# Load tiles moved by 128 bytes, and every load one chunk on two rings

## The chip, the core and the metric

The kernel runs on one core of a Trainium2 chip. The metric is the device time of one execution in microseconds (us). A core has five engines with instruction streams of their own: TensorE (PE, with PEld for its weight loads), VectorE (DVE), ScalarE (ACT), GpSimd (POOL) and SyncE (SP), which only issues transfers here. A transfer (DMA) is issued by an instruction on an engine's queue (SPq, ACTq) and is carried out by 16 DMA engines that all queues share. SyncE's and ScalarE's issues go into a ring each.

## The reference

Four inputs `q`, `k`, `v`, `alpha` of shape (4, 8, 768, 48) in fp32 are 4 batches of 8 heads, 768 steps and 48 numbers. A recurrence over the steps gives `y`, and a mixture of low-rank adapters is added to it:

```
for t in range(S):
    state = alpha[:, :, t, :, None] * state + einsum('bhd,bhe->bhde', k[:, :, t], v[:, :, t])
    y[:, :, t] = einsum('bhd,bhde->bhe', q[:, :, t], state)
x = y.transpose(0, 2, 1, 3).reshape(3072, 384)
logits = x @ w_gate                      # 8 experts, the best two are kept, softmax over them
delta = sum over the two: w * ((x @ A[e]) @ B[e])      # rank 16
return x + delta
```

## The kernel before

**Units.** The work is cut into 24 units: unit u is chunk c = u % 6 (128 steps) of batch b = u // 6, all 8 heads. For a unit ScalarE takes the logarithm of alpha (`ln`), TensorE sums it along the chunk (`cum`), ScalarE exponentiates (`exp`), GpSimd multiplies k and q by that (`kg`, L381) and casts v (`vb`), TensorE transposes (`tr`), ScalarE copies the result out of PSUM (`kq`), TensorE forms the 128x128 attention blocks (`at`), VectorE masks them (`msk`, L412), TensorE multiplies by v and by the state (`av`, `kv`; VectorE scales the state, `st`), ScalarE copies y (`ysb`, L454), TensorE transposes it (`xt`), ScalarE casts it (`xs`). Then groups of one to three units go through the gate: `z`, a chain of small VectorE steps, `zt`, `zs`, and for each unit `dl` and `o` (VectorE adds, L559), after which the unit is stored.

**Order.** The order of all these steps is fixed when the program is built: `_order` plays a list schedule with a cost for each step (`_ops`), a priority for each (`PRIO`, `PERIOD`) and an arrival time for each loaded piece (`_arrivals`). No clock exists when the kernel runs: each engine takes its instructions in that order and waits for semaphores.

**Loads.** `_plan` lists the loads. Batch 0 is loaded by chunk: 24 pieces of 128 steps x 8 heads x 48 numbers, 196,608 bytes each. Batches 1 and 2 and `a`, `k` of batch 3 are loaded whole, 10 loads of six such pieces; `q` and `v` of batch 3 by chunk again. `load` (L266) issues one. Three of the first six go to ScalarE's ring, all others to SyncE's; the three weight loads (`W_st`, `G_st`, `B_st`) come after the 16th load. There are two buffers of each tile (`a_t`, `kq_t`, `v_t`), so a load of batch 2 waits for the readers of batch 0 (`pump`, L569). Stores are issued on SyncE once no load is left in the queue.

**Where the rows lie.** In SBUF a head's 48 numbers (192 bytes) have a slot of 64 numbers (256 bytes), so rows start 256 bytes apart. In the built program `a_t0` begins at byte 16,512 of each partition, which is 64.5 x 256, and the other load tiles follow at multiples of 256 behind it. So each row fills bytes 128 to 319 counted from a multiple of 256: it crosses one such multiple. `W_st` begins at 151,680 (592.5 x 256). It too is loaded in rows of 192 bytes, eight per partition, but these lie one behind the other: they start at 128, 64, 0 and 192 from a multiple of 256, twice over, and half of them cross one. In DRAM the rows of the inputs and of `moe_A` are 192 bytes apart.

**Completion counters.** The framework merges the engines' streams into one order and gives the DMAs in it eight completion counters in turn (`DMAHW0` to `DMAHW7`). A DMA is issued only when the one eight before it in that order, which had the same counter, has landed. At most eight transfers are under way, and an engine whose next instruction is such a DMA waits with all that stands behind it.

Of the kernel before, what the change touches and what calls it, by code (L numbers as in the profile page):

```python
# [18 lines left out]
NCH = S // C  # L19
# [13 lines left out]
LNS = [[0], [1]] + [[u, u + 1] for u in range(2, NU, 2)]  # L33
CAST = set()


# [19 lines left out]
def _pe(t):  # L56
    return t + .22, t


SMALL = (.17, .13)  # L60
KEEP = dict(lg=2, ex=3, kg=4, kt=4, am=3, sb=2, vb=4, xs=9)
SLOTS = dict(C=1, A=1, M=3)
PRIO = dict(ln=5.1, cum=-1.8, exp=10.2, kg=-0.6, vb=2.0, tr=1.7, kq=2.4, at=3.7, msk=-1.3, st=10.4,
            kv=4.1, av=2.5, ysb=17.0, xb=5.0, xt=10.1, xs=-6.3, z=13.4, gm=7.3, df=8.3, ge=8.9,
            gx=19.3, wu=5.0, dn=4.8, w=-0.1, zw=16.1, zt=7.3, zs=20.8, dl=12.7, o=3.4)
PERIOD = 2.6
SLACK = 0.


def _ops(arr):  # L70
    ops = {}

    def add(name, eng, length, deps, war=(), alloc=None, frees=None):
        ops[name] = (eng, length, list(deps), list(war), alloc, frees)

    gof = {u: g for g, us in enumerate(GROUPS) for u in us}
    lof = {u: us for us in LNS for u in us}
    for i, us in enumerate(LNS):
        war = [("cum", u) for u in LNS[i - KEEP["lg"]]] if i >= KEEP["lg"] else []
        add(("ln", us[0]), "ACT", _act(DM * len(us) + 30), [("a", u) for u in us], war)  # L80
    for u in range(NU):
# [22 lines left out]
        if u in CAST:  # L104
            add(("xb", u), "POOL", _gpc(DM), [("ysb", u)])
            add(("xt", u), "PE", _pe(.17), [("xb", u)], alloc="M")
        else:
            add(("xt", u), "PE", _pe(.6), [("ysb", u)], alloc="M")
        p = u - KEEP["xs"]
        add(("xs", u), "ACT", _act(DM), [("xt", u)], [("z", gof[p])] if p >= 0 else [],  # L110
            frees=("xt", u))
    for g, us in enumerate(GROUPS):
# [7 lines left out]
        add(("dn", g), "DVE", SMALL, [("wu", g)])  # L120
        add(("w", g), "DVE", (.32, .28), [("dn", g)])
        add(("zw", g), "DVE", _dve(P * n), [("w", g)], frees=("z", g))
# [8 lines left out]
def _order(arr):  # L131
# [10 lines left out]
    def prio(n):  # L142
        s, i = n
        return (last[i] if s in ("z", "gm", "df", "ge", "gx", "wu", "dn", "w", "zw", "zt", "zs")
                else i) * PERIOD + PRIO[s]

# [54 lines left out]

def _plan():
    plan = []
# [7 lines left out]
    return plan  # L211


def _arrivals(plan):
    t, arr = 2.6, {}
    for x, b, c in plan:
        t += 4.2 if c is None else .75
        for j in (range(NCH) if c is None else (c,)):
            arr[x, b * NCH + j] = t
    return arr  # L220


@with_exitstack
def kernel(
# [12 lines left out]
    plan = _plan()  # L237
    order, slot, _ = _order(_arrivals(plan))

# [44 lines left out]

    queue = list(plan)
    for i in range(6):
        load(queue.pop(0), nc.sync if i % 2 == 0 else nc.scalar)
    load(queue.pop(0), nc.sync)
    load(queue.pop(0), nc.sync)
    for i in range(8):  # L290
        load(queue.pop(0), nc.sync)
    load_weights()

# [267 lines left out]
    RUN = dict(ln=ln, cum=cum, exp=exp, kg=kg, vb=vb, tr=tr, kq=kq, at=at, msk=msk, st=stf, kv=kv,  # L561
               av=av, ysb=ysb, xb=xb, xt=xt, xs=xs, z=z, gm=gm, df=df, ge=ge, gx=gx, wu=wu, dn=dn,
               w=w, zw=zw, zt=zt, zs=zs, dl=dl, o=o)
    READ = dict(a="ln", k="kg", q="kg", v="vb")
    reads = Counter()
    whole = 0
    done = []

    def pump():  # L569
        while queue:  # L570
            x, b, c = queue[0]
            if b > 1 and reads[x, b - 2] < NCH:
                return
            load(queue.pop(0), nc.sync)

# [5 lines left out]
    with tc.manual_schedule():  # L581
        for s, i in order:
            if (s, i) == ("xs", 0):
                cast_weights()
            RUN[s](i)
            for x, r in READ.items():
                if r == s:
                    for u in (LNS[lof[i][0]] if s == "ln" else (i,)):
                        reads[x, u // NCH] += 1
            pump()  # L590
            if s == "o":
                done.append(i)
            if not queue:
                while done:
                    store(done.pop(0))
# [30 lines left out]
```

## Time and profile before

| | us |
|---|---|
| median of 3 runs | 144.97 (144.84 to 145.39) |
| the profiled execution | 145.53 |
| its span in the trace | 143.8 |
| DVE busy | 72.6 |
| ACT busy | 66.8 |
| PE busy | 87.8 |

The span is the time between the first and the last instruction in the trace; 1.7 us of the profiled execution lie around it. Busy time is that in which an engine executes. Issuing a DMA isn't counted as busy.

### The profile page before, as it was taken

How to read it: one execution, taken by the hardware profiler on the slowest of the kernel's cores; microseconds unless marked ns; L12 is line 12 of the kernel's file. 1: busy time of each engine (PE TensorE's matmuls, PEld its weight loads, DVE VectorE, ACT ScalarE, POOL GpSimd, SP SyncE). 2: the span in 40 equal slices, each digit the busy share in tenths (PEclk: the TensorE clock that was granted, in tenths of full speed). 3: DMA queues.
4: the chain of work that ended last, by engine and by line, in shares of the span. 5: the costliest groups of instructions: out<-in, count | busy, mean ns of one | idle time of the engine just before them, and what ended most of it. 6: DMA issues, size and time to landing. Idle time of an engine off the chain costs nothing.

```text
span 143.8 us, 2839 instructions
## 1 busy us (share of the span) xinstructions
PE 87.8 (61%) x1112; PEld 67.3 (47%) x1112; DVE 72.6 (51%) x170; ACT 66.8 (46%) x128; POOL 56.0 (39%) x58
## 2 busy tenths in 40 slices
PE   0236645559629800998199307780995887969560
PEld 0125434337518500766178206650883765957310
DVE  3004306724516550367055501792299399899792
ACT  3323263136258600443596603643687594745410
POOL 4066108314600005959250029592244958540000
PEclk9999999999986975558969955999699999999965
DMA  4999999999999998999997999999988999954036
GB/s 90 165 163 163 163 164 211 149 171 173 160 167 164 167 143 177 160 167 162 171 152 153 160 167 163 163 163 168 163 149 161 172 166 304 372 204 159 5 112 219
DMA packets 57757, 24.18 MB, mean 168 GB/s; under 512 B 39184, under 2 KB 57744, under 8 KB 57744
## 3 DMA queue, kind: packets, MB, share of 16 engines
q1 hardware_dynamic: 54624, 23.41, 98.2%
q10 hardware_dynamic: 3120, 0.59, 3.4%
q8 instruction: 8, 0.13, 0.5%
q14 instruction: 5, 0.04, 0.1%
HBM read 19.28 MB, written 4.72 MB: 167 GB/s over the span
## 4 chain that ended last, share of the span: by engine, by line
SPq 56%; DVE 14%; DMA 12%; PE 10%; issue 3%; ACT 2%; POOL 1%; DVEq 0%; ACTq 0%
SPq L270 36%; SPq L272 18%; DMA a_t<-in_alpha_dram 12%; DVE am L412 3%; DVE o_t L559 3%; DVE w L528 2%; PE M_t L395 2%; POOL kgq L381 1%; DVE zw L535 1%; PE M_t L555 1%; DVE sb L419 1%; SPq L282 1%; SPq L280 1%; DVE mx L493 1%; PE S_t L432 1%
## 5 line engine op out<-in xcount | busy, mean ns | idle before, releaser
L381 POOL TENSOR_TENSOR kgq<-kq_t,ex 128x768 bf16<-128x768 f32 x24 | 43.4, 1820 | 42.4 <-DMA kq_t<-in_q_dram 35.2
L412 DVE TENSOR_TENSOR am<-at_t,mask 128x1024 bf16<-128x1024 f32 x24 | 29.2, 1219 | 13.2 <-PE at_t L407 13.2
L395 PE MATMUL M_t<-ident,kgq 128*128 128x128 bf16 x192 | 19.8, 265 | 16.9 <-POOL kgq L381 16.9
L376 ACT ACTIVATE ex<-cum_t 128x776 f32<-128x776 f32 x24 | 19.7, 820 | 12.2 <-POOL kgq L381 6.0
L419 DVE TENSOR_TENSOR sb<-S_t,ex 128x384 bf16<-128x384 f32 x20 | 11.0, 551 | 27.2 <-PE S_t L432 15.8
L395 PEld LDWEIGHTS <-kgq 128*128 128x128 bf16 x192 | 15.1, 120 | 18.8 <-POOL kgq L381 17.9
L389 POOL CAST vb<-v_t 128x384 bf16<-128x384 f32 x24 | 11.9, 506 | 28.5 <-DMA v_t<-in_v_dram 20.7
L399 ACT COPY kqt<-M_t 128x512 f32<-128x512 f32 x24 | 14.1, 586 | 18.8 <-PE M_t L395 18.3
L360 ACT ACTIVATE lg<-a_t 128x768 bf16<-128x768 f32 (+1 forms) x13 | 10.3, 799 | 22.7 <-DMA a_t<-in_alpha_dram 22.7
L365 PE MATMUL cum_t<-lg,suf 128*128 128x384 bf16 x24 | 9.9, 411 | 16.6 <-ACT lg L360 16.3
L467 PE MATMUL M_t<-ident,o_t 128*128 128x128 f32 x72 | 15.3, 327 | 3.8 <-ACT o_t L454 3.7
L454 ACT COPY o_t<-M_t 128x384 f32<-128x384 f32 x24 | 11.5, 480 | 7.0 <-PE M_t L449 7.0
L472 ACT CAST xs<-M_t 128x384 bf16<-128x384 f32 x24 | 11.5, 480 | 3.2 <-PE M_t L467 3.2
L559 DVE TENSOR_TENSOR o_t<-M_t,o_t 128x384 f32<-128x384 f32 x24 | 12.5, 552 | 0.9 <-PE M_t L555 0.7
L467 PEld LDWEIGHTS M_t<-ident,o_t 128*128 128x128 f32 x72 | 10.7, 203 | 4.5 <-ACT o_t L454 4.3
L407 PE MATMUL at_t<-kqt 48*128 48x128 bf16 x192 | 11.1, 245 | 0.7 <-ACT kqt L399 0.7
L442 PE MATMUL M_t<-sb,kqt 128*128 128x96 bf16 x80 | 7.7, 228 | 4.7 <-ACT xs L472 4.4
L366 PE MATMUL cum_t<-lg,nsuf 128*128 128x384 bf16 x24 | 10.2, 426 | 0.0
L366 PEld LDWEIGHTS <-nsuf 128*128 128x128 bf16 x24 | 2.6, 109 | 15.9 <-issue 15.7
L432 PEld LDWEIGHTS <-kgq 128*128 128x128 bf16 x80 | 6.4, 111 | 7.4 <-issue 4.2
L449 PE MATMUL M_t<-vb,am 128*128 128x48 bf16 x192 | 9.7, 193 | 0.1
L432 PE MATMUL S_t<-vb,kgq 128*128 128x96 bf16 x80 | 7.8, 228 | 3.0 <-POOL kgq L381 2.1
(47 smaller groups left out, 108.1 us busy)
## 6 DMA issues: line engine op xcount, KB each, us to landing
out_dram<-o_t SPq DMA_DIRECT2D x24, 192.0 KB, 2.9
kq_t<-in_q_dram SPq DMA_DIRECT2D x12, 192.0 KB, 5.3
v_t<-in_v_dram SPq DMA_DIRECT2D x11, 192.0 KB, 5.2
a_t<-in_alpha_dram SPq DMA_DIRECT2D x6, 192.0 KB, 5.2
kq_t<-in_k_dram SPq DMA_DIRECT2D x4, 192.0 KB, 5.3
kq_t<-in_k_dram ACTq DMA_DIRECT2D x2, 192.0 KB, 6.3
v_t<-in_v_dram ACTq DMA_DIRECT2D x1, 192.0 KB, 6.4
W_st<-in_moe_A_dram SPq DMA_DIRECT2D x1, 192.0 KB, 4.9
```

What stands on the lines that cost most here:

```text
L270: eng.dma_start(out=t[:, :, 0:D], in_=src.rearrange("h (c j) d -> j (h c) d", j=C))
L272: eng.dma_start(out=view(t)[:, c], in_=src[:, c * C:(c + 1) * C, :].rearrange("h j d -> j h d"))
L366: nc.tensor.matmul(cum_t[:, N0:D0], nsuf[:, :], t[:, :, 0:D], start=True, stop=True)
L376: nc.scalar.activation(st["ex"][u], cum_t[:, U0:D0 + 2 * NP], AF.Exp)
L381: nc.gpsimd.tensor_tensor(out=kgq[u % KEEP["kg"]][:, :, :, 0:D], in0=src, in1=st["ex"][u][:, 0:2 * DM].rearrange("p (w h d) -> p w h d", w ...
L395: nc.tensor.transpose(t[:, w, p, :], pair(kgq[u % KEEP["kg"]][:, w], p), ident[:, :])
L399: nc.scalar.copy(t, bank("tr", u)[:, :])
L412: nc.vector.tensor_tensor(out=st["am"][u].rearrange("p a b t -> p (a b) t"), in0=at_t.rearrange("p a b t -> p (a b) t"), in1=_bc_mid(mask[ ...
L419: nc.vector.tensor_tensor(out=st["sb"][u].rearrange("p a b d -> p (a b) d"), in0=S_t.rearrange("p a b d -> p (a b) d"), in1=_bc(st["ex"][u ...
L432: nc.tensor.matmul(S_t[:, p].rearrange("p b d -> p (b d)"), pair(kgq[u % KEEP["kg"]][:, 0], p), pair(st["vb"][u], p), start=(c == 0 and p ...
L467: nc.tensor.transpose(t[:, i * P:(i + 1) * P], x[:, i, :], idn[:, :])
L559: nc.vector.tensor_tensor(out=o_t[u], in0=bank("dl", u)[:, 0:DM], in1=o_t[u], op=ALU.add)
```

## The change

One 128-byte tile, `row_start`, is allocated ahead of the load tiles, and all SBUF addresses behind it move by 128: `a_t0` now begins at 16,640 (65 x 256), so a load row fills bytes 0 to 191 from a multiple of 256. The plan is one piece of one tensor at a time, in order of use, for all four batches: 96 loads. They alternate between the rings: `a` and `q` on SyncE, `k` and `v` on ScalarE. ScalarE's loads (`ld`) become steps of the list schedule, each due `LEAD` = 5 us ahead of its planned arrival and placed in ScalarE's instruction stream among its activations. SyncE's are held back by the same due times where the program is written out. The weights follow the 20th load. Some costs and all priorities of the planner have new values.

```diff
+LEAD = 5.
+FIRST = 6
+def _ring(i, item):
+    return "ACT" if i % 2 else "SP"
-SMALL = (.17, .13)
+SMALL = (.2, .09)
-PRIO = dict(ln=5.1, cum=-1.8, exp=10.2, kg=-0.6, vb=2.0, tr=1.7, kq=2.4, at=3.7, msk=-1.3, st=10.4,
+PRIO = dict(ln=-7.3, cum=15.0, exp=18.0, kg=-14.7, vb=67.1, tr=-5.5, kq=10.8, at=-13.4, msk=15.8,
...
-PERIOD = 2.6
+PERIOD = 3.0
+def _plan():
+    plan = []
+    for u in range(NU):
+        b, c = divmod(u, NCH)
+        plan += [(x, b, c) for x in "akqv"]
+    return plan
+def _arrivals(plan):
+    t, arr = 2.6, {}
+    for i, (x, b, c) in enumerate(plan):
+        t += 4.2 if c is None else .75
+        for j in (range(NCH) if c is None else (c,)):
+            arr[x, b * NCH + j] = t
+        arr["due", i] = t - LEAD
+    return arr
+    prev = []
+    for i, (x, b, c) in enumerate(_plan()):
+        if i >= FIRST and _ring(i, (x, b, c)) == "ACT":
...
+            add(("ld", i), "ACT", (.5, .45), [("due", i)], war + prev)
+            prev = [("ld", i)]
-    for c in range(NCH):
-        plan += [("a", 0, c), ("k", 0, c), ("q", 0, c), ("v", 0, c)]
-    for b in (1, 2):
-        plan += [(x, b, None) for x in "akqv"]
-    plan += [("a", 3, None), ("k", 3, None)]
-    for c in range(NCH):
-        plan += [("q", 3, c), ("v", 3, c)]
+    big.tile([P, 32], F4, name="row_start")
+    for i in range(FIRST):
+        load(queue.pop(0)[1], nc.sync if _ring(i, plan[i]) == "SP" else nc.scalar)
+    rings = {r: [x for x in queue if _ring(*x) == r] for r in ("SP", "ACT")}
+    def ld(i):
+        assert rings["ACT"][0][0] == i
+        load(rings["ACT"].pop(0)[1], nc.scalar)
+    weights = 20
-            if b > 1 and reads[x, b - 2] < NCH:
+            if arr["due", i] > now or any(
+                    (b - 2) * NCH + j not in reads[x]
+                    for j in (range(NCH) if c is None else (c,)) if b > 1):
                 return
-            load(queue.pop(0), nc.sync)
+            load(q.pop(0)[1], nc.sync)
```

SyncE's queue where batch 1 is loaded, before: whole tensors of batch 1 into the second buffers, then those of batch 2 (a name's ending number is its serial number; a row in brackets names the semaphores waited for).

```order
L270 DMA a_t1_87<-in_alpha_dram 128x48x48 [waits DMAHW3_49]
L270 DMA kq_t1_89<-in_k_dram 128x48x48 [waits DMAHW4_49]
L270 DMA kq_t1_89<-in_q_dram 128x48x48 [waits DMAHW5_49]
L270 DMA v_t1_91<-in_v_dram 128x48x48 [waits DMAHW6_49]
L270 DMA a_t0_86<-in_alpha_dram 128x48x48 [waits DMAHW7_49,Activation_49]
```

SyncE's queue at the same place of the change, from the weights on.

```order
L298 DMA W_st_117<-in_moe_A_dram 128x8x48 [waits DMAHW0_49]
L300 DMA G_st_118<-in_moe_w_gate_dram 128x24 [waits DMAHW2_49]
L301 DMA B_st_119<-in_moe_B_dram 128x384 [waits DMAHW3_49]
L290 DMA a_t0_87<-in_alpha_dram 128x8x48 [waits DMAHW4_49]
L290 DMA kq_t0_89<-in_q_dram 128x8x48 [waits DMAHW6_49]
L290 DMA a_t1_88<-in_alpha_dram 128x8x48 [waits DMAHW0_49]
L290 DMA kq_t1_90<-in_q_dram 128x8x48 [waits DMAHW1_49]
```

`k` and `v` have left SyncE's queue, and the pieces that stay are a sixth of a whole load.

ScalarE's stream at its first logarithms, before.

```order
L360 ACTIVATE lg0_141<-a_t0_86 128x8x48 [waits DMAHW0_49]
L376 ACTIVATE ex_201<-cum_t_173 128x776 [waits PE_49]
L360 ACTIVATE lg1_142<-a_t0_86 128x8x48 [waits DMAHW3_49]
L376 ACTIVATE ex_222<-cum_t_173 128x776 [waits PE_49]
L399 COPY kqt_228<-M_t0_176 128x512 [waits PE_49]
```

The same place in the change.

```order
L374 ACTIVATE lg0_129<-a_t0_87 128x8x48 [waits DMAHW0_49]
L290 DMA v_t0_91<-in_v_dram 128x8x48
L390 ACTIVATE ex_179<-cum_t_161 128x776 [waits PE_49]
L290 DMA kq_t0_89<-in_k_dram 128x8x48 [waits DMAHW4_49]
L374 ACTIVATE lg1_130<-a_t0_87 128x8x48 [waits DMAHW3_49]
L290 DMA v_t0_91<-in_v_dram 128x8x48 [waits DMAHW7_49]
L390 ACTIVATE ex_205<-cum_t_161 128x776 [waits PE_49]
L290 DMA kq_t0_89<-in_k_dram 128x8x48 [waits DMAHW1_49]
L413 COPY kqt_215<-M_t0_164 128x512 [waits PE_49]
```

Between two activations there now stands a DMA issue with a wait for a landing of its own.

ScalarE's stream at its last load, in the change (unit 23's v; `o_t16` is `ysb` of unit 16).

```order
L290 DMA kq_t1_90<-in_k_dram 128x8x48 [waits DMAHW5_49]
L468 COPY o_t15_108<-M_t0_164 128x384
L390 ACTIVATE ex_1402<-cum_t_161 128x776 [waits DVE_49,Pool_49]
L290 DMA v_t1_92<-in_v_dram 128x8x48 [waits DMAHW6_49]
L524 ACTIVATE xe_1429<-M_t1_165 128x24 [waits DVE_49,PE_49]
L468 COPY o_t16_109<-M_t2_166 128x384 [waits PE_49]
L486 CAST xs_1442<-M_t0_164 128x384 [waits PE_49]
L390 ACTIVATE ex_1451<-cum_t_161 128x776 [waits PE_49,Pool_49]
```

Before, the copy of unit 16 stands between a logarithm and a copy, and no load is near it.

```order
L360 ACTIVATE lg0_141<-a_t1_87 128x16x48 [waits Activation_49]
L454 COPY o_t16_108<-M_t0_176 128x384 [waits DVE_49,PE_49]
L399 COPY kqt_1388<-M_t1_177 128x512 [waits DVE_49,PE_49]
L472 CAST xs_1399<-M_t2_178 128x384 [waits DVE_49,PE_49]
L454 COPY o_t17_109<-M_t1_177 128x384 [waits PE_49]
```

All 45 loads of ScalarE that follow its first three now stand ahead of its copy of unit 16. In the merged order the last of them, v of unit 23, is the 111th DMA and waits for the landing of the 103rd, which is the store of unit 9. The first 103 are 90 of the 96 loads, the three weights and ten stores: SyncE, whose 48 loads are then all issued, stores what is ready.

## Rows read from the trace of the kernel before

**Rows 1.** The page: engines' busy time and two of its 40-slice rows.

```profile
PE 87.8 (61%) x1112; PEld 67.3 (47%) x1112; DVE 72.6 (51%) x170; ACT 66.8 (46%) x128; POOL 56.0 (39%) x58
...
DMA  4999999999999998999997999999988999954036
...
GB/s 90 165 163 163 163 164 211 149 171 173 160 167 164 167 143 177 160 167 162 171 152 153 160 167 163 163 163 168 163 149 161 172 166 304 372 204 159 5 112 219
```

**Rows 2.** The page: bytes moved over the whole span.

```profile
HBM read 19.28 MB, written 4.72 MB: 167 GB/s over the span
```

**Rows 3.** The page: the chain that ended last, shares by engine.

```profile
SPq 56%; DVE 14%; DMA 12%; PE 10%; issue 3%; ACT 2%; POOL 1%; DVEq 0%; ACTq 0%
```

**Rows 4.** The view of waits: total us, times, longest us.

```profile
POOL kgq L381 <- DMA kq_t<-in_q_dram: 35.2, 4, 17.3
...
ACT lg L360 <- DMA a_t<-in_alpha_dram: 22.7, 7, 4.5
...
POOL vb L389 <- DMA v_t<-in_v_dram: 20.7, 7, 4.2
```

**Rows 5.** SyncE's queue in time: start us, us, engine, line, DMA.

```profile
0.80 0.44 SPq L272 DMA_DIRECT2D a_t<-in_alpha_dram  x1
...
2.84 1.97 SPq L272 DMA_DIRECT2D kq_t<-in_q_dram  x1
...
4.85 2.36 SPq L272 DMA_DIRECT2D v_t<-in_v_dram  x1
...
16.91 1.14 SPq L272 DMA_DIRECT2D v_t<-in_v_dram  x1
...
18.10 1.14 SPq L280 DMA_DIRECT2D W_st<-in_moe_A_dram  x1
...
31.59 6.77 SPq L270 DMA_DIRECT2D kq_t<-in_k_dram  x1
...
115.92 1.14 SPq L272 DMA_DIRECT2D v_t<-in_v_dram  x1
```

**Rows 6.** The DMA view, 17 to 30 us: forty slices of 0.325 us.

```profile
GB/s 163 165 164 162 163 163 165 159 164 167 162 161 164 171 202 241 258 249 249 275 178 162 166 156 181 175 154 66 92 135 220 169 102 168 219 148 170 185 150 134
```

**Rows 7.** The DMA view, issues around 18 us: last column us to landing.

```profile
v_t<-in_v_dram SPq DMA_DIRECT2D x1, 192.0 KB, 5.2
...
W_st<-in_moe_A_dram SPq DMA_DIRECT2D x1, 192.0 KB, 4.9
```

**Rows 8.** ScalarE in time at the start (ACTq is its sequencer).

```profile
0.80 1.28 ACT L251 ACT_TABLE_LOAD   x1 [0.80 <-PEq L610]
...
0.83 0.48 ACTq L272 DMA_DIRECT2D kq_t<-in_k_dram  x1
...
2.07 1.32 ACTq L272 DMA_DIRECT2D kq_t<-in_k_dram  x1
...
4.73 0.52 ACT L360 ACTIVATE lg<-a_t 128x384 bf16<-128x384 f32 x1 [2.65 <-DMA a_t<-in_alpha_dram]
```

**Rows 9.** VectorE in time: two of its mask products, late in the program.

```profile
119.84 1.22 DVE L412 TENSOR_TENSOR am<-at_t,mask 128x1024 bf16<-128x1024 f32 x1
...
131.52 1.22 DVE L412 TENSOR_TENSOR am<-at_t,mask 128x1024 bf16<-128x1024 f32 x1
```

**Rows 10.** Busy us (and instructions) of each engine in two stretches.

```profile
core 0: us, PE busy (x) PEld busy (x) DVE busy (x) ACT busy (x) POOL busy (x), PEclk, DMA share, GB/s
...
112.80:143.80 31.00, 22.08 (x311) 16.43 (x308) 25.07 (x70) 15.91 (x37) 10.56 (x9) 0.90 0.76 191
...
120.00:130.00 10.00, 8.84 (x144) 7.15 (x142) 9.61 (x20) 6.64 (x15) 5.28 (x4) 1.00 0.82 291
```

**Rows 11.** GpSimd in time: the first and the last of its 24 products.

```profile
7.27 1.81 POOL L381 TENSOR_TENSOR kgq<-kq_t,ex 128x768 bf16<-128x768 f32 x1 [4.95 <-DMA kq_t<-in_q_dram]
...
125.73 1.82 POOL L381 TENSOR_TENSOR kgq<-kq_t,ex 128x768 bf16<-128x768 f32 x1 [1.74 <-ACT ex L376]
```

**Rows 12.** ScalarE in time: its copy of unit 16.

```profile
112.82 0.48 ACT L454 COPY o_t<-M_t 128x384 f32<-128x384 f32 x1 [2.19 <-PE M_t L449]
```

More of the change, by code (lines that the diff above doesn't have):

```diff
@@ L77, in _ops @@
     lof = {u: us for us in LNS for u in us}
+    prev = []
+    for i, (x, b, c) in enumerate(_plan()):
+        if i >= FIRST and _ring(i, (x, b, c)) == "ACT":
+            war = []
+            for j in (range(NCH) if c is None else (c,)):
+                u = (b - 2) * NCH + j
+                if u >= 0:
+                    war.append(dict(a=("ln", lof[u][0]), k=("kg", u), q=("kg", u), v=("vb", u))[x])
+            add(("ld", i), "ACT", (.5, .45), [("due", i)], war + prev)
+            prev = [("ld", i)]
     for i, us in enumerate(LNS):
@@ L107, in _ops @@
         else:
-            add(("xt", u), "PE", _pe(.6), [("ysb", u)], alloc="M")
+            add(("xt", u), "PE", _pe(.38), [("ysb", u)], alloc="M")
         p = u - KEEP["xs"]
@@ L120, in _ops @@
         add(("dn", g), "DVE", SMALL, [("wu", g)])
-        add(("w", g), "DVE", (.32, .28), [("dn", g)])
+        add(("w", g), "DVE", (.4, .29), [("dn", g)])
         add(("zw", g), "DVE", _dve(P * n), [("w", g)], frees=("z", g))
@@ L143, in prio @@
         s, i = n
+        if s == "ld":
+            return i - 999.
         return (last[i] if s in ("z", "gm", "df", "ge", "gx", "wu", "dn", "w", "zw", "zt", "zs")
@@ L199, in _bc_mid @@
                    ap=aps[:1] + [[0, r] for r in reps] + aps[1:])
-def _plan():
-    plan = []
-    for c in range(NCH):
-        plan += [("a", 0, c), ("k", 0, c), ("q", 0, c), ("v", 0, c)]
-    for b in (1, 2):
-        plan += [(x, b, None) for x in "akqv"]
-    plan += [("a", 3, None), ("k", 3, None)]
-    for c in range(NCH):
-        plan += [("q", 3, c), ("v", 3, c)]
[L211 to L220, printed above, removed]
 @with_exitstack
@@ L237 @@
     plan = _plan()
-    order, slot, _ = _order(_arrivals(plan))
+    arr = _arrivals(plan)
+    order, slot, when = _order(arr)
     big = ctx.enter_context(tc.tile_pool(name="big", bufs=1))
@@ L283, in load_weights @@
         nc.sync.dma_start(out=B_st, in_=moe_B.rearrange("e r f -> (e r) f"))
-    queue = list(plan)
-    for i in range(6):
-        load(queue.pop(0), nc.sync if i % 2 == 0 else nc.scalar)
-    load(queue.pop(0), nc.sync)
[L289 to L292, printed above, removed]
+    queue = list(enumerate(plan))
+    for i in range(FIRST):
+        load(queue.pop(0)[1], nc.sync if _ring(i, plan[i]) == "SP" else nc.scalar)
+    rings = {r: [x for x in queue if _ring(*x) == r] for r in ("SP", "ACT")}
     suf = consts.tile([P, P], F2, name="suf")
@@ L564, with pump @@
     READ = dict(a="ln", k="kg", q="kg", v="vb")
-    reads = Counter()
-    whole = 0
+    reads = defaultdict(set)
+    weights = 20
     done = []
-    def pump():
-        while queue:
-            x, b, c = queue[0]
-            if b > 1 and reads[x, b - 2] < NCH:
+    def pump(now):
+        q = rings["SP"]
+        while q:
+            i, (x, b, c) = q[0]
+            if arr["due", i] > now or any(
+                    (b - 2) * NCH + j not in reads[x]
+                    for j in (range(NCH) if c is None else (c,)) if b > 1):
                 return
-            load(queue.pop(0), nc.sync)
+            load(q.pop(0)[1], nc.sync)
     def store(u):
@@ L588 @@
                     for u in (LNS[lof[i][0]] if s == "ln" else (i,)):
-                        reads[x, u // NCH] += 1
-            pump()
+                        reads[x].add(u)
+            pump(when[s, i][0])
+            if weights and len(plan) - len(rings["SP"]) - len(rings["ACT"]) >= weights:
+                load_weights()
+                weights = None
             if s == "o":
                 done.append(i)
-            if not queue:
+            if not rings["SP"] and not rings["ACT"]:
                 while done:
```

11 lines of the change are left out of this document (6 added, 5 removed).

## The prediction

> **What bounds the kernel now.** I read the page first. No engine is the bound: VectorE is busy half of the span and TensorE 61%, but the 16 DMA engines are all but full from the second slice to the thirty-third, about 3.6 to 118 us, at some 165 GB/s [rows 1]. The chain that ended last agrees: 56% of it lies on SyncE's queue and 12% on a transfer [rows 3]. 19.28 MB read at 165 GB/s are 117 us [rows 2]. The view of waits tells what that does: GpSimd's product waits 35.2 us for q, ScalarE's logarithm 22.7 us for alpha and GpSimd's cast 20.7 us for v [rows 4]. So for 118 us the kernel waits for loads, and the last 26 us are work that the loads left behind.
>
> What a load costs: at 163 GB/s one piece of 196,608 bytes takes r = 1.20 us. The slices of 30 to 97 us, where whole tensors are loaded, scatter (143 to 177 GB/s) about the same value as those of the pieces before [rows 1], so cutting a whole load into six pieces is priced at nothing; nor did the two rings at the start move more than SyncE's alone later (90, 165, 163 and on, [rows 1]). Only a different r can shorten the loads.
>
> **The rows' place.** `W_st` is the one load of the trace with the same row of 192 bytes and the same spacing in DRAM, but other places in SBUF: half of its rows cross a multiple of 256, where all rows of the other loads do. The v piece ahead of it was issued at 16.91 and landed 5.2 us later, at 22.1; `W_st` was issued at 18.10 and landed after 4.9 us, at 23.0 [rows 5, 7]. The slices of that time read 202, 241, 258 and 249 GB/s against 160 to 167 ahead of them [rows 6]. By the landings 196,608 bytes took 0.9 us, by the slices 0.8; I use 0.85 instead of 1.20. So where a row lies in SBUF counts, and r after the change has two ends. The upper is 0.85: the gain of `W_st` and no more, as if what is left were the reading, which doesn't change. The lower is the fastest that anything moves here, 372 GB/s while only stores run [rows 1]: 0.53 us. It is also about what follows if crossing explains all of the difference, since (1.20 + x) / 2 = 0.85 gives x = 0.50. No row tells reading from crossing, so I take the middle, r = 0.70.
>
> The Trainium skill has a rule for this (DMA: Bandwidth & Descriptors, section How a descriptor splits into AXI transactions): a transfer is cut at multiples of 256 bytes, and one that starts off such a multiple also pays for the bytes below its start. By it a row now costs 8 + 2 = 10 beats and then 6, r would be 1.20 x 6/10 = 0.72 us, an estimate, and the sum below would be 108.4 us instead of 106.6. The trace agrees only in part: by the same count the rows of `W_st` cost 9 beats on average, so 1.08 us, and it took 0.85.
>
> **The sum.** Two paths can set the end.
>
> The compute path: what is the pace of a unit if its data are there? From 119.84 to 131.52 us VectorE ran four units, 2.92 us each [rows 9], and was busy 9.61 of 10 us [rows 10]; the last load was issued at 115.92 [rows 5], so by some 121 us all data were there. The first product of GpSimd started at 7.27 and the last at 125.73, 18.1 us ahead of the end [rows 11]. So this path is 7.27 + 23 x 2.92 + 18.1 = 92.5 us. The new priorities reorder the same instructions, and I price that at nothing: hidden by the loads as long as the pace stays under 3.5 us, where this path would reach the other.
>
> The load path: ScalarE's last load, v of unit 23, now stands ahead of its copy of unit 16 and waits for the 103rd DMA. If the loads are slower than the computation, ScalarE is held there until 103 DMAs have landed. That is 4.7 us for the first (its logarithm starts at 4.73, [rows 8]), 89 more pieces, the weights, about 405 KB at the 245 GB/s of [rows 6] or 1.65 us, and ten stores at 0.53 us, 5.3 us. All that then still has to be done is what stood behind the copy of unit 16 before: it started at 112.82 [rows 12], and from there to the end are 31.0 us, with VectorE busy 25.07 of them [rows 10]. I take 31.0; 25.1 is the other end. Behind the held ScalarE stand the exponentials and copies of units 16 to 23, and TensorE and VectorE wait for these. With r = 0.70 the path is 4.7 + 62.3 + 1.65 + 5.3 + 31.0 = 104.9 us. It is the longer one, so the span is 104.9 us, and with the 1.7 us around it (145.5 - 143.8) the execution takes 106.6, rounded to **107 us**. The profiled execution is 0.4% above the median; I leave that within the rounding. With r = 0.85 it is 118.3 + 1.7 = 120 us; with r = 0.53 the load path falls to 89.8, the compute path decides and the time is 94.2 us.
>
> What each part costs besides. SyncE loses 45 of its load issues to ScalarE. Such an issue occupies the queue for 0.44 us where nothing blocks it, and 1.97 to 2.36 us where it waits for room [rows 5]; on ScalarE it was 0.48 and, blocked, 1.32 us, and the first one ran inside the table load, 0.83 to 1.31 within 0.80 to 2.08 [rows 8]. So an issue takes ScalarE's sequencer, not its datapath. ScalarE is busy 66.8 us in all [rows 1], less the table load 2.73 us per unit; two issues of 0.48 fit beside that as long as a unit takes 3.1 us or more, and I price them at nothing. What hides them is the activation ahead, and the price without this cover is in a rival below. Loading in order of use removes the wait for whole tensors: the q of a whole load cost GpSimd 17.3 us at worst [rows 4]. That isn't a term of its own, since both paths already assume data in order. The padding itself is no instruction.
>
> **The rivals.**
>
> *The rows' place does nothing; `W_st` was faster because its rows lie one behind the other, which load rows never do.* For it: no row separates the two. Against: nothing in the trace shows that gaps cost, either. Then r stays 1.20, the load path is 4.7 + 106.8 + 1.65 + 5.3 + 31.0 = 149.5, and the time 151 us, slower than before: ScalarE, held by its loads, would start the last eight units later than now, since the loads that SyncE alone issued never stood in its way. It decides from r = 1.13 on, where the path reaches 143.8. I give this 10%.
>
> *ScalarE's issues aren't hidden.* Each then costs its 0.48 us, a unit takes ScalarE 2.73 + 0.96 = 3.69 us, and the compute path becomes 7.27 + 84.9 + 18.1 = 110.2, so 112 us. For it: blocked issues of 1.32 us are in the trace. Against: the issue inside the table load. 12%, and inside the range.
>
> *Compute alone decides*, because r is near 0.53: 94 us. It is the lower end of my forecast: for it speaks the 372 GB/s, against it the 0.85 of `W_st`, whose reads are the same.
>
> **How the numbers follow.** The forecast, r between 0.53 and 0.85 with the load path or compute in command, gets 72% and runs from 94 to 120 us; hidden issues failing gets 12% at 112; no effect gets 10% at 151; 6% is left for what I don't see, of either sign. The range of 94 to 120 us leaves out the 10%, and half of the 6% and the forecast's margins, in all about 2 in 10. Runs of this kernel spread by 0.4%, so half a per cent is about what can be told from no change. Slower by more gets 8% (most of the no-effect case), the same 2%, faster 90%.
>
> **What would show it.** The slices of DMA during the loads: 270 to 290 GB/s if r is 0.70, 163 if the place does nothing. ScalarE's waits: if the load path decides, its issues wait on its own queue in the last third of the loads, and its copy of unit 16 starts near 74 us with 31 us to go; if compute decides, the loads finish early, the DMA slices show gaps and VectorE is busy nine tenths. SyncE's stores should start before ScalarE's last loads. The prediction is wrong if r is outside 0.53 to 0.85, if the issues lengthen ScalarE's units past 3.5 us, or if what follows the last load is far from 31 us.

## The result and the profile after

| | us | ratio to before, 95% |
|---|---|---|
| before, median of the runs beside it | 144.91 (144.84 to 145.39) | |
| changed kernel, median of 4 runs | 124.14 (123.08 to 124.76) | 0.855 (0.849 to 0.862) |
| its profiled execution | 124.76, span 123.1 | |

A run over 1.5% longer than the fastest of its kernel is left out of the medians and ratios, here and below, so that e6 and e7 rest on one run each, while the expectations quote medians of all runs.

The kernel became 14% faster. The forecast was 107 us, the range 94 to 120: right in its sign, 17 us too low, and the time lies outside the range.

The page of the changed kernel, its lines for [rows 1 to 3]: busy time of the engines, two rows of 40 slices (3.08 us each), bytes, and the shares of the chain.

```profile
PE 83.5 (68%) x1112; PEld 64.7 (53%) x1112; DVE 68.9 (56%) x170; ACT 66.6 (54%) x128; POOL 56.3 (46%) x58
...
DMA  3999999998999999999999998997985031050055
GB/s 75 258 259 257 259 273 259 258 232 175 243 259 208 195 258 253 217 258 235 192 259 259 320 271 173 184 279 146 248 202 114 0 140 60 5 192 0 3 196 187
...
HBM read 19.28 MB, written 4.72 MB: 195 GB/s over the span
...
DMA 23%; DVE 22%; PE 20%; SPq 19%; ACT 7%; issue 4%; ACTq 2%; DVEq 1%; POOL 0%; POOLq 0%
```

The dense slices read 259 GB/s where they read 163 before: a piece of 196,608 bytes now takes 0.76 us instead of 1.20. But from the ninth slice on the row dips again and again, down to 146 before the last load is issued at 91 us: the transfers are faster, and no longer back to back. The chain is no longer mainly one engine's: transfers, VectorE, TensorE and SyncE's queue have about a fifth each.

The view of waits of the changed kernel, for [rows 4] (total us, times, longest):

```profile
POOL kgq L395 <- ACT ex L390: 33.4, 14, 6.1
...
POOL vb L403 <- DMA v_t<-in_v_dram: 5.5, 2, 3.7
```

GpSimd's product no longer waits for q (35.2 us before) but for the exponential: 33.4 us. So why is ScalarE late? ScalarE in time, the six instructions ahead of which it idled longest on a transfer (in brackets, us), with what stands ahead of the second; ACTq is its own queue:

```profile
10.08 0.82 ACT L390 ACTIVATE ex<-cum_t 128x776 f32<-128x776 f32 x1 [2.75 <-DMA a_t<-in_alpha_dram]
...
24.28 0.59 ACT L413 COPY kqt<-M_t 128x512 f32<-128x512 f32 x1 [1.38 <-PE M_t L409]
29.61 0.40 ACTq L290 DMA_DIRECT2D kq_t<-in_k_dram  x1
30.14 0.82 ACT L390 ACTIVATE ex<-cum_t 128x776 f32<-128x776 f32 x1 [5.27 <-DMA kq_t<-in_q_dram]
...
40.31 0.59 ACT L413 COPY kqt<-M_t 128x512 f32<-128x512 f32 x1 [3.67 <-DMA a_t<-in_alpha_dram]
...
49.91 0.48 ACT L468 COPY o_t<-M_t 128x384 f32<-128x384 f32 x1 [3.12 <-DMA a_t<-in_alpha_dram]
...
59.23 0.19 ACT L524 ACTIVATE xe<-M_t 128x24 f32<-128x24 f32 x1 [3.39 <-DMA kq_t<-in_q_dram]
...
69.63 0.48 ACT L468 COPY o_t<-M_t 128x384 f32<-128x384 f32 x1 [2.86 <-DMA kq_t<-in_q_dram]
```

None of these reads q or alpha; an exponential of `cum_t` and copies out of PSUM read what TensorE wrote. They stand still because just ahead of each is one of ScalarE's own loads. The six add up to 21.1 us.

Take the second. ScalarE came to the k load of unit 7 at 24.9 us. Eight places ahead of it in the merged order stands q of unit 8, on SyncE's ring, and that landed at 29.6. The exponential of unit 4, which needs neither, stands behind the load, and ScalarE idled for 5.27 us ahead of it. The issue itself took 0.40.

ScalarE again, at its last load and the copy of unit 16 [rows 12]; SyncE's queue at its last load and first stores; three of GpSimd's products, those of units 9, 13 and 23 [rows 11]; and busy time by windows, for [rows 10] (the DMA share adds up the time of packets that overlap, so it can exceed 1):

```profile
91.27 0.92 ACTq L290 DMA_DIRECT2D v_t<-in_v_dram  x1
...
92.71 0.48 ACT L468 COPY o_t<-M_t 128x384 f32<-128x384 f32 x1
```

```profile
64.82 0.50 SPq L290 DMA_DIRECT2D kq_t<-in_q_dram  x1
65.41 2.43 SPq L600 DMA_DIRECT2D out_dram<-o_t  x3
```

```profile
53.85 1.82 POOL L395 TENSOR_TENSOR kgq<-kq_t,ex 128x768 bf16<-128x768 f32 x1
...
76.34 1.82 POOL L395 TENSOR_TENSOR kgq<-kq_t,ex 128x768 bf16<-128x768 f32 x1 [0.73 <-ACT ex L390]
...
105.52 1.82 POOL L395 TENSOR_TENSOR kgq<-kq_t,ex 128x768 bf16<-128x768 f32 x1
```

```profile
core 0: us, PE busy (x) PEld busy (x) DVE busy (x) ACT busy (x) POOL busy (x), PEclk, DMA share, GB/s
...
3.00:24.00 21.00, 12.60 (x131) 9.11 (x131) 6.13 (x9) 9.16 (x15) 9.56 (x9) 1.00 1.27 260
...
92.70:123.10 30.40, 22.98 (x318) 17.06 (x316) 24.48 (x67) 17.15 (x38) 12.63 (x10) 0.88 0.26 88
24.00:95.00 71.00, 50.11 (x697) 40.28 (x696) 39.31 (x88) 41.02 (x78) 34.38 (x31) 0.86 1.06 227
```

From the copy of unit 16 to the end are 30.4 us, where 31.0 were forecast. So what is missing was lost ahead of it: the copy started at 92.7 and not at 74. SyncE was through its loads at 65 us, ScalarE issued its last one at 91. From 24 to 95 us the transfers averaged 227 GB/s, stores included, after 260.

The products tell where it was lost. From unit 13 (76.34) to unit 23 (105.52) they came 2.92 us apart, the pace that the forecast gave to a unit whose data are there. From the first (6.38) to that of unit 13 they came 5.38 us apart, and the six waits fall into that stretch. At its last load ScalarE wasn't held: the DMA which that load waits for, the store of unit 9, was issued at 86.67 and landed 2.4 us later, and ScalarE came to the load at 91.27.

```profile
86.67 0.33 SPq L600 DMA_DIRECT2D out_dram<-o_t  x1
```

```profile
out_dram<-o_t SPq DMA_DIRECT2D x1, 192.0 KB, 2.4
```

### The profile page after: what moved, and what is told of

Its sections match the earlier page's. It is cut to its first block, busy times and chain, and to the rows that moved or that the text cites. A ratio compares the mean times of both kernels' runs of the same rounds, so it can differ in the third digit from the quotient of the medians.

```text
span 123.1 us, 2905 instructions
## 1 busy us (share of the span) xinstructions
PE 83.5 (68%) x1112; PEld 64.7 (53%) x1112; DVE 68.9 (56%) x170; ACT 66.6 (54%) x128; POOL 56.3 (46%) x58
## 2 busy tenths in 40 slices
DMA packets 104638, 24.19 MB, mean 197 GB/s; under 512 B 101424, under 2 KB 104624, under 8 KB 104624
## 4 chain that ended last, share of the span: by engine, by line
DMA 23%; DVE 22%; PE 20%; SPq 19%; ACT 7%; issue 4%; ACTq 2%; DVEq 1%; POOL 0%; POOLq 0%
SPq L290 19%; DMA kq_t<-in_q_dram 12%; DMA a_t<-in_alpha_dram 8%; DVE o_t L577 5%; DVE am L426 5%; PE M_t L481 4%; PE M_t L409 3%; DMA W_st<-in_moe_A_dram 3%; DVE sb L433 3%; DVE w L542 3%; PE at_t L421 2%; DVE zw L549 2%; PE M_t L500 2%; ACTq L290 2%; ACT ex L390 2%
## 5 line engine op out<-in xcount | busy, mean ns | idle before, releaser
L395 POOL TENSOR_TENSOR kgq<-kq_t,ex 128x768 bf16<-128x768 f32 x24 | 43.5, 1818 | 33.5 <-ACT ex L390 33.4
L390 ACT ACTIVATE ex<-cum_t 128x776 f32<-128x776 f32 x24 | 19.8, 823 | 13.4 <-DMA kq_t<-in_q_dram 5.3
L433 DVE TENSOR_TENSOR sb<-S_t,ex 128x384 bf16<-128x384 f32 x20 | 11.0, 551 | 18.7 <-ACT ex L390 13.4
L409 PE MATMUL M_t<-ident,kgq 128*128 128x128 bf16 x192 | 16.9, 240 | 4.1 <-ACT o_t L468 2.7
L379 PE MATMUL cum_t<-lg,suf 128*128 128x384 bf16 x24 | 9.0, 373 | 12.2 <-ACT lg L374 6.5
L409 PEld LDWEIGHTS <-kgq 128*128 128x128 bf16 x192 | 13.5, 109 | 5.7 <-issue 3.8
L421 PEld LDWEIGHTS <-kqt 48*128 48x128 bf16 x192 | 6.2, 102 | 15.4 <-ACT kqt L413 12.3
L569 PE MATMUL M_t<-B_all,zs 128*128 128x384 bf16 x24 | 8.1, 365 | 1.9 <-DVE zw L549 0.7
L380 PE MATMUL cum_t<-lg,nsuf 128*128 128x384 bf16 x24 | 9.2, 384 | 0.0
L463 PEld LDWEIGHTS <-am 128*128 128x128 bf16 x192 | 8.1, 105 | 0.8 <-DVE am L426 0.4
```

The costliest lines, as they stand in the source:

```text
L390: nc.scalar.activation(st["ex"][u], cum_t[:, U0:D0 + 2 * NP], AF.Exp)
L395: nc.gpsimd.tensor_tensor(out=kgq[u % KEEP["kg"]][:, :, :, 0:D], in0=src, in1=st["ex"][u][:, 0:2 * DM].rearrange("p (w h d) -> p w h d", w ...
L409: nc.tensor.transpose(t[:, w, p, :], pair(kgq[u % KEEP["kg"]][:, w], p), ident[:, :])
L421: nc.tensor.matmul(at_t[:, hh, p, :], kq[rows, 0, p, :], kq[rows, 1, p, :], start=True, stop=True)
L433: nc.vector.tensor_tensor(out=st["sb"][u].rearrange("p a b d -> p (a b) d"), in0=S_t.rearrange("p a b d -> p (a b) d"), in1=_bc(st["ex"][u ...
L463: nc.tensor.matmul(y[:, h * D:(h + 1) * D], st["am"][u][:, hh, p, :], st["vb"][u][:, h, :], start=(c == 0 and h == 0), stop=(h == H - 1), ...
```

## The experiments

All are edits of the kernel before or of the changed one; times are medians, with the range of all runs in brackets.

| run | us | ratio to before, 95% |
|---|---|---|
| e1 rows' place alone | 111.8 (111.3 to 113.9) | 0.768 (0.761 to 0.776) |
| e2 all but the place | 156.3 (156.2 to 156.6) | 1.072 (1.064 to 1.080) |
| e3 SyncE issues all | 125.5 (124.8 to 128.8) | 0.861 (0.851 to 0.871) |
| e4 loads later | 122.8 (122.1 to 123.4) | 0.842 (0.835 to 0.849) |
| e5 in step | 124.9 (124.2 to 125.7) | 0.858 (0.851 to 0.865) |
| e6 only v on ScalarE | 114.2, one run (114.2 to 119.3) | not given |
| e7 place, new table | 116.3, one run (116.3 to 118.6) | not given |
| e9 change, old table | 125.8 (125.5 to 127.7) | 0.867 (0.858 to 0.877) |
| e10 only v, old table | 114.0 (113.2 to 115.5) | 0.786 (0.776 to 0.797) |
| e12 SyncE all, old table | 126.1 (124.5 to 126.5) | 0.864 (0.855 to 0.873) |
| e14 v earlier | 114.7 (114.3 to 116.1) | 0.790 (0.785 to 0.795) |
| e11 mixed | 113.0 (111.6 to 113.4) | 0.777 (0.768 to 0.785) |
| e13 mixed, q and v cut | 112.2 (110.9 to 112.7) | 0.770 (0.764 to 0.777) |
| e15 rows at byte 64 | 113.1 (113.0 to 113.3) | 0.779 (0.773 to 0.784) |
| e16 rows at byte 192 | 145.3 (144.6 to 146.6) | 1.003 (0.998 to 1.007) |
| e17 rows at byte 32 | 112.9 (112.3 to 113.5) | 0.777 (0.769 to 0.785) |

### The place alone, and everything but the place

```diff
+    big.tile([P, 32], F4, name="row_start")     # e1: added to the kernel before
-    big.tile([P, 32], F4, name="row_start")     # e2: taken out of the changed one
```

> The kernel before, with only the row_start tile added: whole loads on SyncE's queue as before, every row now at a multiple of 256 bytes. If the rows' place alone makes the transfers faster, the slices of the 16 DMA engines rise from about 165 to about 255 GB/s, as in the changed kernel, and the time falls: 96 loads x (1.20 - 0.76) = 42 us off 145 us gives 103, up to 112 if SyncE's queue then waits for buffers. If the place does nothing and the changed kernel's gain is from its order and its two rings, the time stays at 145 us and the slices at 165 GB/s.

> The changed kernel without the row_start tile: cuts, order and both rings as in it, rows at their old places. If the place is what shortens a piece (1.20 us back in place of 0.76), the loads alone take 95 x 1.20 + 6.4 = 120 us and some 20 us of compute follow: 138 to 150 us, no faster than before. If the rings or the order bring the gain, the time stays near 124 us and the slices near 255 GB/s.

The 40 slices of e1 (2.81 us each) and of e2 (3.86 us each), with e1's packets:

```profile
GB/s 45 259 258 221 203 208 210 166 215 261 203 217 240 263 124 125 298 247 209 293 214 313 251 210 317 234 264 204 165 201 200 317 355 255 218 163 48 21 220 182
DMA packets 57757, 24.18 MB, mean 215 GB/s; under 512 B 39184, under 2 KB 57744, under 8 KB 57744
```

```profile
GB/s 101 163 163 163 163 170 198 163 168 163 125 184 165 166 148 179 163 165 165 163 168 156 170 164 163 251 247 155 176 226 170 236 117 52 107 4 153 2 102 204
```

One tile of 128 bytes a partition, with every load, ring and priority left as it was, makes the kernel 23% faster. It alone beats the whole change by 12 us. Without it the rest of the change makes the kernel 7% slower than before: 163 GB/s is back, and ScalarE is tied to the loads. The forecast's rival "the rows' place does nothing" is this case, and gave 151 us for it; my expectation for e2, 138 to 150, was too low as well.

### Where must a row lie?

```diff
-    big.tile([P, 32], F4, name="row_start")
+    big.tile([P, 48], F4, name="row_start")     # e15: 192 bytes; e16: 16 (64 bytes); e17: 40 (160)
```

> The kernel before with 192 bytes ahead of the load tiles in place of none: every row of 192 bytes now fills bytes 64 to 255 of its 256, crossing no multiple of 256 and starting at a multiple of 64. If only crossing costs, the dense slices read 259 GB/s (0.76 us a piece) and the time is about 112 us, as with rows at 0. If rows must start at a multiple of 256, they read less, 165 to 220 GB/s.

> The kernel before with 64 bytes ahead of the load tiles: every row starts at byte 192 and runs 128 bytes into the next 256. If crossing alone sets the price, the slices read 163 GB/s and the time is 145 us, as with rows at 128; if the number of 64-byte blocks on either side counts too, another rate.

> The kernel before with 160 bytes ahead of the load tiles: every row fills bytes 32 to 223 of its 256, crossing no multiple of 256 but starting off a multiple of 64. If only crossing costs: 259 GB/s and about 112 us. If the start must be a multiple of 64, the slices read less than 240 GB/s.

Each as an edit of e1. The slices of e15, e16 and e17:

```profile
GB/s 43 259 259 219 222 211 241 133 207 242 232 261 241 295 172 299 243 240 280 143 278 218 299 193 248 224 216 212 157 203 206 285 367 327 155 178 34 35 214 177
```

```profile
GB/s 93 165 163 163 163 164 205 137 179 167 163 163 163 168 162 162 163 164 163 170 162 169 163 164 163 163 163 168 163 152 168 163 173 276 369 247 160 5 114 218
```

```profile
GB/s 45 259 259 213 216 207 206 129 216 223 261 73 292 211 296 207 250 281 233 299 213 280 286 167 307 165 295 211 175 196 206 289 368 326 155 152 59 12 232 181
```

Where pieces are loaded without a gap, in the second and third slice, rows at 0, 32 and 64 read 259 GB/s, rows at 128 (before) and at 192 read 163. At these five places only whether a row crosses a multiple of 256 counts, not where it starts and not how its bytes divide. The Trainium skill (DMA: Bandwidth & Descriptors, section How a descriptor splits into AXI transactions) counts beats of 32 bytes and charges the bytes below an unaligned start: 6, 7 and 8 beats for rows at 0, 32 and 64, 10 and 12 for rows at 128 and 192. The trace doesn't agree: the first three cost the same 0.76 us a piece and the last two the same 1.20. The section speaks of what a transaction reads; what was moved here is the place that is written.

### Loads off ScalarE, later, in step

```diff
-        load(rings["ACT"].pop(0)[1], nc.scalar)  # e3
+        load(rings["ACT"].pop(0)[1], nc.sync)
-LEAD = 5.                                        # e4
+LEAD = 1.
-    weights = 20
+    weights = 16
+            if rings["ACT"] and rings["ACT"][0][0] < i:   # e5, in pump
+                return
```

> The changed kernel with ScalarE's 45 in-stream loads issued by SyncE at the same places of the program; every instruction of compute stands where it stood. Theory: ScalarE's program is held by its own loads, each of which waits for an earlier transfer to land, and its exponentials and copies come late behind them; then the holds go, the transfers run without gaps (96 x 0.76 + 6 us: last load landed near 80 us) and the end is 17 to 20 us after that, 97 to 104 us. Rival: the order of the work (the new table of priorities) or the pace of compute sets 124 us, and the time stays within 4 us of it, with the last kgq still near 105 us.

> The changed kernel with LEAD 1 in place of 5: each load stands some 4 us later in the program (the weights after 16 loads instead of 20, so that they still come ahead of their use). Theory of the held ScalarE: by the time that ScalarE comes to a load, the transfer that it waits for has landed, so ScalarE's waits on transfers shrink and the time falls below 120 us, unless the transfers now start too late, which would show as slices under 200 GB/s with ScalarE's loads issued without a wait. Rival, that the order of the work sets the time: 124 us within 3.

> The changed kernel, but SyncE issues a load only after every ScalarE load that stands ahead of it in the order of use. Theory of the rings that run apart: in the changed kernel SyncE's a and q land up to 25 us ahead of their use, while the k and v of the units in work wait their turn, and what the transfers win goes into the wrong pieces; then k and v of unit 9 land near 36 us in place of 43.6 and 45.6, and the time falls to 108 to 118 us. Theory of the held ScalarE: its waits on landings stay, SyncE now waits with it, and the time is 122 to 132 us.

e3 went against my theory: ScalarE's holds were gone, and the time was no better. The rival's figure was met, for another reason than the rival's, as the next section shows. e4 halved the holds (9.8 us by the waits) and brought a little over 1 us, where the two intervals touch (0.849): not the 120 us or less of the theory, and within the 3 us of its rival. Now pieces came late. Its waits show v, 21.7 us against 5.5:

```profile
POOL vb L403 <- DMA v_t<-in_v_dram: 21.7, 7, 5.4
```

e5 turned out to be no experiment: the loads were already written in that order, the edit left every instruction in its place, and the run only repeats the changed kernel. SyncE runs ahead at run time, where nothing in the program holds it. So no run tests the theory of the rings that run apart, but the trace of the changed kernel bears on it. For unit 9 alpha landed at 30.4 us and k at 43.6, 13 us behind, so the rings do run apart; yet its product started 10 us after that k (53.85, shown above). These are the k load and its time to landing:

```profile
39.85 0.41 ACTq L290 DMA_DIRECT2D kq_t<-in_k_dram  x1
```

```profile
kq_t<-in_k_dram ACTq DMA_DIRECT2D x1, 192.0 KB, 3.7
```

In units 4 to 23 the last of a unit's four pieces landed 8.5 to 15.7 us ahead of its product. The units are not late for want of data. The rings' running apart can still cost time in another way: the piece that a load of ScalarE waits for is often one of a later unit, as q of unit 8 for k of unit 7.

### How much on ScalarE, under both tables

```diff
-    return "ACT" if i % 2 else "SP"
+    return "ACT" if i % (2 if i < FIRST else 4) == (1 if i < FIRST else 3) else "SP"
```

This is e6, the changed kernel with v alone on ScalarE. e7 is e1 with the new SMALL, PRIO, PERIOD and the four other new costs; e9 is the changed kernel with the old ones; e10 is e6 and e12 is e3 with the old ones.

> The changed kernel with ScalarE taking only the v pieces after the first six loads, SyncE a, q and k. Theory: two costs stand against each other, ScalarE held by its own loads (some 17 us of the run without in-stream loads that the other ring's missing share hid) and a single ring that carries cut pieces at about 1.0 us each; with a quarter on ScalarE both shrink: SyncE's 71 pieces take 71 us at 1.0 us, ScalarE is held half as often, and the time falls to 110 to 118 us. If instead the time of the changed kernel is set by neither (by the table of the order), it stays at 122 to 127 us.

> The kernel before with the row_start tile and, beyond that, the changed kernel's table of priorities, period and costs; whole loads on SyncE's queue. If the new table costs or gains nothing by itself, 111 us as with the old table, within 3. If the new table is what keeps the changed kernel at 124 us, this one moves to 116 us or more. Against the run in which SyncE issued all cut loads (126.6 us) it also tells what the cut costs on one ring: 111 us here would put 15 us on it.

> The changed kernel (place, cuts, both rings) with the old table of priorities, period and costs. The new table cost 6 us with whole loads on one ring (118.2 against 112.3 us). If that is a property of the table, this run is some 6 us below the changed kernel: 118 us. If the new table suits the new order of arrivals and only misfits the old one, it is 124 us or more.

> ScalarE takes only the v pieces and the old table stands. If the costs of the ring, of ScalarE's holds and of the table add, this run is 118 - 6 = 112 us; if the table does nothing here, 118 us. ScalarE's exponentials should start within 4 us of the landing of their a piece up to the last.

> All cut loads after the first six on SyncE's ring, old table: with the two runs of the same table (v alone on ScalarE 114.4, k and v on ScalarE 126.8) it makes a row of three. Theory of two opposed costs: one ring carries cut pieces at about 1.0 us, so the last lands near 98 us and the time is 117 to 122 us, above the run with v on ScalarE and below the one with k and v. If a single ring costs nothing and only ScalarE's holds do, it is 112 us or less. Waits of kgq on exponentials below 20 us, of lg on its a piece above 20 us.

| share of the loads on ScalarE | new table | old table |
|---|---|---|
| none in the stream | 125.5 (e3) | 126.1 (e12) |
| v alone | 114.2 (e6, one run) | 114.0 (e10) |
| k and v | 124.1 (the change) | 125.8 (e9) |
| none, whole loads | 116.3 (e7, one run) | 111.8 (e1) |

The waits of e9, with all of ScalarE's that its next activation doesn't read; then those of e10, then of e12:

```profile
POOL kgq L394 <- ACT ex L389: 33.8, 14, 5.1
...
ACT o_t L467 <- DMA kq_t<-in_q_dram: 4.5, 1, 4.5
ACT ex L389 <- DMA a_t<-in_alpha_dram: 4.4, 2, 2.9
ACT kqt L412 <- DMA kq_t<-in_q_dram: 3.5, 2, 2.8
ACT xs L485 <- DMA kq_t<-in_q_dram: 3.0, 1, 3.0
```

```profile
POOL kgq L394 <- ACT ex L389: 18.4, 10, 4.8
...
ACT lg L373 <- DMA a_t<-in_alpha_dram: 14.8, 9, 2.8
```

```profile
ACT lg L373 <- DMA a_t<-in_alpha_dram: 23.5, 11, 4.3
POOL vb L402 <- DMA v_t<-in_v_dram: 20.3, 11, 5.1
POOL kgq L394 <- ACT ex L389: 17.5, 8, 5.8
```

SyncE's queue in e12, two of its issues, and in e1, two of its whole loads:

```profile
35.42 0.76 SPq L289 DMA_DIRECT2D a_t<-in_alpha_dram  x1
...
82.84 2.52 SPq L289 DMA_DIRECT2D a_t<-in_alpha_dram  x1
```

```profile
43.03 4.03 SPq L271 DMA_DIRECT2D a_t<-in_alpha_dram  x1
...
66.03 4.20 SPq L271 DMA_DIRECT2D kq_t<-in_k_dram  x1
```

```profile
GB/s 88 206 203 302 329 313 321 254 151 136 303 314 305 322 319 244 60 104 243 313 298 315 319 284 162 195 158 294 326 318 319 338 172 154 248 310 314 318 318 290
```

Two costs stand against each other. With everything on SyncE's ring, the 48 cut pieces from alpha of unit 9 to alpha of unit 21 take 47.4 us, 0.99 each, though SyncE does nothing but issue; whole loads on the same ring take 4.60 us for six pieces (five in 23.0 us), 0.77 each. That is a mean: the slices of e1 from 43 to 66 us (0.575 us each) go in bursts of 294 to 338 GB/s, faster than the 259 of cut pieces, with dips to 60 between the loads. So then the data are late: ScalarE waits 23.5 us for its alpha. With k and v on ScalarE the pieces go at 0.76 where nothing stops them, and it is ScalarE that is late: 15.4 us of its waits are for landings that the next activation doesn't read, and GpSimd waits 33.8 us for exponentials. With v alone no such wait is left, and the time is 12 us lower (0.867 and 0.786). That pair, e9 and e10, moves k loads only, and moves them to the ring that suffers from more. Nor do earlier data explain the gain: in units 4 to 23 of e9 the last piece of a unit landed 7.1 to 14.2 us ahead of its product, in e10 0.8 to 8.1. So it has to come from ScalarE.

The table of priorities does not explain the 124 us: with the old one the changed kernel takes 1.6 us more (the intervals overlap), e12 0.5 us more than e3, e10 0.2 us less than e6, and e1 4.5 us less than e7, the last two against one run each. The expectation that costs add (112) was met within 2 us for e10. That of e12 (117 to 122) missed by 4, and not by the ring's price: that was taken as 1.0, and the last piece, forecast near 98 us, landed at 98.65. What followed it took 25.7 us, more than I had allowed.

### Loads moved up in ScalarE's program

e14 is e10 with each v load moved up to eight activations ahead in ScalarE's program, after the last use of its place.

```diff
     order, slot, when = _order(arr)
+    for n in [n for n in order if n[0] == "ld"]:
+        x, b, c = plan[n[1]]
+        stop = ("vb", (b - 2) * NCH + c)
+        j = order.index(n)
+        order.remove(n)
+        passed = 0
+        while j and passed < 8 and order[j - 1][0] != "ld" and order[j - 1] != stop:
+            j -= 1
+            passed += order[j][0] in ("ln", "exp", "kq", "ysb", "xs", "gx", "zs")
+        order.insert(j, n)
```

> As the run with v alone on ScalarE and the old table (114.4 us); only ScalarE's v loads stand up to eight activations earlier in its program (not ahead of the last use of their place), all else in the same order and every load on the same ring. Theory of the held ScalarE: standing earlier, each comes before the transfer that it waits for has landed, ScalarE's exponentials and copies stand still behind it, and the time rises by 4 us or more, with 10 us or more of ScalarE's waits on transfers that its next activation doesn't read (none in the run compared with). Rival, that only the share of the rings counted and a held ScalarE costs nothing because its data are late anyway: 114 us within 2.

```profile
ACT lg L383 <- DMA a_t<-in_alpha_dram: 8.0, 5, 2.3
ACT lg L383 <- DMA v_t<-in_v_dram: 7.4, 1, 7.4
```

The rival's 114 us came, and not the rise of 4 us or more. But only one hold came of the edit, 7.4 us ahead of the first logarithm, where 10 us or more were meant, so it leaves the question open and sets a limit to the theory. The median rose by 0.7 us: the first exponential was 5.5 us later than in e10, the product of unit 4 1.6 us (28.2 against 26.6), since from there on the loads set the pace and ScalarE's waits for alpha fell by as much (14.8 to 8.0). By this one hold a held ScalarE is free where the data come later still; it can cost time only where it is what the others wait for.

### Can both be beaten?

e11 cuts the first two batches (v on ScalarE), loads the third whole and the fourth as before; e13 cuts q and v of the third too. Both have the old table.

```diff
-    for u in range(NU):
+    for u in range(2 * NCH):
         b, c = divmod(u, NCH)
         plan += [(x, b, c) for x in "akqv"]
+    plan += [(x, 2, None) for x in "akqv"]       # e13: a and k whole, q and v by chunk, for b = 2 and 3
+    plan += [("a", 3, None), ("k", 3, None)]
+    for c in range(NCH):
+        plan += [("q", 3, c), ("v", 3, c)]
```

> A version meant to beat both: the first two batches cut (v on ScalarE, the rest on SyncE), the third whole, of the last a and k whole and q and v cut; rows at multiples of 256 bytes; old table. By the landings of the runs so far 48 pieces at 0.88 us end at 44 us, the whole loads at 0.77 a piece at 72, the last cut ones at 82 to 86; the twelfth kgq stands near 54 us, 11 more at 2.75 us and 18 us of remainder give 102 to 108 us. If cut pieces in the first half are what makes the changed kernel late, there is no gain over the 112 us of the run with whole loads.

> As the mixed version (113.1 us), but q and v of the third batch cut too, since there kgq of unit 12 waited 10.7 us for the whole q load: a and k whole (4.6 us each) end near 54 us, q of unit 12 lands at 55 in place of 59, and the remaining units follow at 2.75 us: 55 + 30 + 18 to 21 = 104 to 108 us. If cut pieces cost again what the earlier start wins, 111 to 114 us.

Both beat the changed kernel by 11 to 12 us, but not e1: 0.777 and 0.770 against 0.768, within the intervals. The 102 to 108 us that I had added up from the earlier start did not arrive, and why is not shown.

## Why the prediction was wrong

- **The bound (loads at 163 GB/s): right.** e1 changes nothing but where the tiles lie, and gains 23%.
- **The place shortens a piece: right. r = 0.70: 8% too low.** It is 0.76. On 89 pieces that is 5.3 us. I took the middle between 0.53 and 0.85 because no row told reading from crossing; e15 to e17 show that pieces whose rows don't cross take 0.76, wherever the rows start. `W_st` misled me: half of its rows cross, the middle of 1.20 and 0.76 is 0.98, and it took 0.85 to 0.9. Why it was faster is not shown. The beats of the Trainium skill gave 0.72, nearer, by a count that the same runs contradict.
- **"ScalarE is held there until 103 DMAs have landed": the step that failed.** It took the DMAs to run back to back up to the copy of unit 16. With r = 0.76 that would be 4.7 + 67.6 + 1.65 + 5.3 = 79.3 us; it started at 92.7. These 13.4 us are the larger part of the miss. I let the loads hold ScalarE at one place near the end and not in between. It was the other way round: at the last load ScalarE was not held (the 103rd DMA had landed at 89.1), and its loads hold it from the first units on (21.1 us by 70 us). Its exponentials and the units come late, and its next loads, which stand behind its own computation, come late too. Each side waits for the other, and the transfers show gaps from 25 us on. So the end was set by the compute path, which the forecast put at 92.5 us: its pace of 2.92 us a unit held from unit 13 on, and the 13 units ahead took 5.38 each. In e2, with r back at 1.20, the same step is 5.7 us off (the copy of unit 16 at 124.2 for 118.5).
- **"Two issues of 0.48 fit beside" the activations: right of the issue (0.37 to 0.40 unblocked), wrong of what goes before it.** What stops ScalarE is the wait for a landing ahead of the issue. The rival on issues that aren't hidden had the right place, but priced the issue alone, 112 us. The 3.1 us a unit in that sentence follows from no row.
- **Cutting whole loads, and the two rings: priced at nothing, wrong once r is small.** At 1.20 us a piece one ring keeps up, and that was what the rows of before showed; at 0.76 a ring with cut pieces does not (0.99), and with whole loads it does on average (0.77). The limit was hidden under the slower transfers. The Trainium skill (DMA: Bandwidth & Descriptors, section Issuing engines are not separate DMA queues) says that issuing from several engines saves only the issue's time. The trace doesn't bear that out: an issue that nothing blocks took 0.37 to 0.40 us, less than a piece, and the second ring still took a cut piece from 0.99 to 0.76 us where both were busy.
- **The remainder of 31.0 us: right** (30.4), and so was the one behind the last product, 17.6 us for 18.1. SyncE's stores did start ahead of ScalarE's last loads (65.4 and 91.3).
- **Reordering at nothing: not quite.** The new table took between 1.6 us less and 4.5 us more than the old one (the latter against one run), depending on the loads beside it.

Open: how the 13.4 us divide between ScalarE standing still and its loads being issued late. e4 traded one for the other, and no run kept half of the loads on each ring without either. Why one ring needs 0.99 us for a cut piece was seen and not explained. TensorE's granted clock was 0.86 on average from 24 to 95 us in the changed kernel and 0.93 from 24 to 88 us in e10; what that adds is not shown either.

## What to carry to other kernels

Before you rebuild the order of loads, look where their rows lie: here one spacer of 128 bytes gave 23%, and all the rest of the change gave part of it back. A load on a computing engine's queue cost that engine here less by its issue (0.37 to 0.40 us) than by the wait ahead of it (2.8 to 5.3 us at six places), and everything behind in its program waits along; give such a queue only as many loads as it can issue without waiting. When you take a bound away, price what it was hiding: steps that were free under 1.20 us a piece were not at 0.76.

## What the runs showed that I had not expected

- Rows of 192 bytes at 256-byte spacing, in cut pieces: 259 GB/s at offsets 0, 32 and 64, 163 GB/s at 128 and 192, with nothing between.
- Whole loads came in fewer packets: 57,757 in e1 (39,184 under 512 bytes) against 104,638 in the changed kernel, by its page:

```profile
DMA packets 104638, 24.19 MB, mean 197 GB/s; under 512 B 101424, under 2 KB 104624, under 8 KB 104624
```

  The ten whole loads have 61,440 rows of 192 bytes. If all of the packets from 512 bytes to 2 KB but the 3,200 of stores and `B_st` are theirs, that is 15,360, one for four rows.
- A single ring carried cut pieces at 0.99 us each and whole loads at 0.77, two rings cut pieces at 0.76. Whole loads went in bursts of 294 to 338 GB/s with dips between, where cut pieces stayed near 259.
